# Retention and GELU MLP on one core: an opening with masks made on chip, earlier casts of v, and another order of loads

## The chip, the cores and the metric

The kernel runs on one core of a Trainium2 chip. The metric is device time in microseconds (us) of one execution; lower is better. Engines are called PE (TensorE matmul), PEld (its weight load), DVE (VectorE), ACT (ScalarE), POOL (GpSimd) and SP (SyncE, which here only issues DMAs).

## The reference

q, k, v are float32 of shape (4 batches, 8 heads, 768 positions, 64). With one decay per head, `gamma = 1 - 2**(-5 - h)`, the first part is a recurrence over positions:

```python
state = gamma * state + einsum('bhd,bhe->bhde', k[:, :, t], v[:, :, t])
y[:, :, t] = 0.125 * einsum('bhd,bhde->bhe', q[:, :, t], state)
```

y, as x of 3072 tokens by 512, goes through a two-layer network with w_in (512 x 2048) and w_out (2048 x 512):

```python
h = x @ w_in
g = 0.5 * h * (1 + tanh(sqrt(2 / pi) * (h + 0.044715 * h ** 3)))
out = g @ w_out
```

## The kernel before

**Chunks.** The positions are cut into six chunks of 128. Within a chunk and batch the recurrence becomes matrix products in float16: transposed q and k give scores (`mm_A`), the scores are multiplied by a triangular mask that also carries a factor per head (`ev_A`, DVE, line 267), the result times v plus the state's contribution gives y (`mm_yi`, `mm_yc`; copied to `xT` by `ev_Y`), and k times v updates the state (`mm_s`, `ev_S`). Powers of gamma are put into q and k while these are cast to float16 (`prep1`, line 177 on DVE or POOL; v is only cast, line 172 on ACT, 174 on POOL). `decay` scales a copy of the state on POOL.

**Two ways to the transposes.** For chunks 0 and 1, PE transposes q and k against an identity matrix (`mm_T`), and `ev_T` copies the result out of PSUM. From chunk 2 for q, and chunk 3 for k, the load itself puts blocks of 32 in place (`load_blk`, 16 DMAs), POOL scales them (`prep_blk`, line 188) and DVE transposes them (line 240).

**The network.** M1 (`moe1`, `moe1_two`, line 401) multiplies w_in by `xT` into banks with tag "h"; GELU on ACT (line 416) gives g. M2 (`moe2`, line 434) multiplies g by w_out; `ev_O` copies the output and sends it out. The eight PSUM banks are two for tag "h", two for "o", four for "att". M1 of chunk 0 is done by pairs of 128-wide column blocks (`fp` 0 to 3, for the token columns `t01` of batches 0 and 1, or the other half), and then by single blocks 8 to 15 for all tokens.

**Order.** The schedule is manual: on every engine and queue, instructions run in the order in which the program lists them. Loads of chunk 0 are issued from SP and ACT, weights from POOL's queue (`load_w_in`, five pieces; `load_w_out`, four), between POOL's `prep1` calls. In the opening PE also runs matmuls on zeros (`spin`). Line 500 builds the mask on DVE: eight `tensor_scalar` instructions that scale a triangle loaded as a constant; the identity matrix is loaded too. `hold` writes one element of the first q tile of chunk 1 from the third piece of w_out, so that chunk 1's loads on SP wait for that piece to land. M2 of chunk 0 is interleaved by hand with the attention of chunk 1, and so on: a dictionary says after which unit of matmul work which attention step is issued. `load(2)` issues chunk 2's loads on SP behind the output DMAs of chunk 0, k and v of each batch in turn; `prep(2, b)` on POOL does q, k, v of each batch in turn.

Of the kernel before, what the change touches and what calls it, by code (L numbers as in the profile page):

```python
# [10 lines left out]
F32 = mybir.dt.float32  # L11
AF = mybir.ActivationFunctionType
ALU = mybir.AluOpType
# [3 lines left out]
def kernel(  # L17
# [9 lines left out]
    nc = tc.nc  # L27
    B, H, S, Dh = q.shape
    C = 128
    NCk = S // C  # L30
    NHP = H // 2
# [8 lines left out]
    p_i = np.arange(128, dtype=np.float64)  # L40
    qdec = gam[None, :] ** (p_i[:, None] - 32.0) * 0.125
    kdec = gam[None, :] ** (160.0 - p_i[:, None])
    g128 = gam ** 128.0
    gst = np.where(p_i[:, None] < 64, g128[None, 0::2], g128[None, 1::2])
    tri = (p_i[:, None] <= p_i[None, :]).astype(np.float64)

    j_p, t_p = np.arange(128)[:, None] // 64, np.arange(128)[:, None] % 32
    hp_c, a_c = np.arange(16)[None, :] // 4, np.arange(16)[None, :] % 4
    g_t, t_t = gam[2 * hp_c + j_p], a_c * 32.0 + t_p
    qdec_t = g_t ** (t_t - 32.0) * 0.125  # L50
    kdec_t = g_t ** (160.0 - t_t)
    cst_np = np.concatenate([qdec, kdec, gst, tri, qdec_t, kdec_t], axis=1).astype(np.float32)
    cst_h = nc.inline_tensor(cst_np, name="rr_cst")
    iden_np = np.eye(128, dtype=np.float32).astype(np.dtype("float16"))
    iden_h = nc.inline_tensor(iden_np, name="rr_ident")

    ctx.enter_context(tc.manual_schedule())
    const = ctx.enter_context(tc.tile_pool(name="const", bufs=1))
# [5 lines left out]
    op = ctx.enter_context(tc.tile_pool(name="op", bufs=4))  # L64
    psum = ctx.enter_context(tc.tile_pool(name="psum", bufs=1, space=bass.MemoryType.PSUM))

    OQ, OK, OG, OT = 0, H, 2 * H, 2 * H + NHP
    OQT, OKT = OT + 128, OT + 144


    misc = const.tile([128, 32], F32)
    cst = const.tile([128, 192], F32)
    iden = const.tile([128, 128], F16)

    raw = {}
# [4 lines left out]
    BLK = {"q": (2, 3, 4, 5), "k": (3, 4, 5)}  # L80
# [20 lines left out]
    def load1(eng, nm, c, b):  # L101
        eng.dma_start(
            out=ld_tile(nm, c, b),
            in_=srcs[nm][b, :, c * C:(c + 1) * C, :].rearrange("h p d -> p h d"),
        )

    def load_blk(nm, c):
        t = ld_all((nm + ("32" if nm == "q" else "T32"), c))
        src = srcs[nm].rearrange("b (hp j) s (dd d) -> j dd s (b hp) d", j=2, dd=2)
        for j in range(2):  # L110
            for dd in range(2):
                for a in range(4):
                    p0, t0 = (2 * j + dd) * 32, c * C + a * 32
                    nc.sync.dma_start(
                        out=t[p0:p0 + 32, :, a, :], in_=src[j, dd, t0:t0 + 32]
                    )

    def load(c):
        for nm in "qk":
            if c in BLK[nm]:  # L120
                load_blk(nm, c)
        for b in range(B):
            for nm in "vk" if c in BLK["k"] else "kv":
                load1(nc.sync, nm, c, b)

    def hold(nm, c, b, until):

        nc.gpsimd.tensor_copy(out=ld_tile(nm, c, b)[0:1, 0, 0:1], in_=until)

    nc.sync.dma_start(out=cst[:, :OT], in_=cst_h.ap()[:, :OT])  # L130
    load1(nc.scalar, "q", 0, 0)
    load1(nc.sync, "k", 0, 0)
    load1(nc.scalar, "k", 0, 1)
    nc.sync.dma_start(out=iden, in_=iden_h.ap())
    nc.sync.dma_start(out=cst[:, OT:OKT + 16], in_=cst_h.ap()[:, OT:])
    load1(nc.sync, "q", 0, 1)
    load1(nc.scalar, "v", 0, 0)
    load1(nc.sync, "k", 0, 2)
# [4 lines left out]

    zero = const.tile([128, 512], F16, name="zero")
    nc.vector.memset(zero, 0.0)  # L145
    nc.scalar.activation(
        out=misc[:, 0:1], in_=zero[:, 0:1], func=AF.Gelu_apprx_tanh, scale=1.0
    )
# [7 lines left out]


    st = const.tile([128, NHP, B, 128], F16, name="st")
    nc.gpsimd.memset(st, 0.0)
    stg = const.tile([128, NHP, B, 128], F32, name="stg")  # L160

    h16 = {}
# [2 lines left out]
    def prep1(eng, nm, c, b):  # L165
        t = pre.tile(
            [128, H, Dh], F16, tag=f"{nm}16", bufs=6 if nm == "q" else 2 * B, name=f"{nm}16"
        )
        src = ld_tile(nm, c, b)
        if nm == "v":  # L170
            if eng is nc.scalar:
                eng.copy(out=t, in_=src)  # L172
            else:
                eng.tensor_copy(out=t, in_=src)  # L174
        else:
            col = OQ if nm == "q" else OK
            eng.tensor_tensor(  # L177
                out=t,
                in0=src,
                in1=cst[:, col:col + H].unsqueeze(2).broadcast_to([128, H, Dh]),  # L180
                op=ALU.mult,
            )
        h16[nm, c, b] = t
# [65 lines left out]
    def mm_A(c, b):  # L249
        t = qkT[c, b]  # L250
        ps = [bank("att", name=f"a_ps{j}") for j in range(2)]
        for hp in range(NHP):
            for j in range(2):
                nc.tensor.matmul(  # L254
                    out=ps[j][:, hp],
                    lhsT=t[j * 64:(j + 1) * 64, 1, hp],
                    rhs=t[j * 64:(j + 1) * 64, 0, hp],
                    start=True,
                    stop=True,
                )  # L260
        pss["A", c, b] = ps

    def ev_A(c, b):
        ps = pss.pop(("A", c, b))
        for j in range(2):
            s = att.tile([128, NHP, 128], F16, tag=f"a{j}", name=f"a_sb{j}")
            nc.vector.tensor_tensor(out=s, in0=ps[j], in1=mask[:, j], op=ALU.mult)  # L267
            a_sb[c, b, j] = s
# [173 lines left out]
    def moe2(c, b, fcs, tag="o"):  # L442
        if fcs[0] == 0:
            o_ps[c, b] = bank(tag, shape=(128, d_model), name="o_ps")
        moe2_mm(o_ps[c, b], c, b, fcs, 0, d_model)

    def ev_O(c, b):
        ps = o_ps[c, b]
        rows = out[b * S + c * C:b * S + (c + 1) * C, :]
        o_sb = op.tile([128, d_model], F32, tag="o", name="o_sb")  # L450
        if b == B - 1 and c > 0:
            nc.vector.tensor_copy(out=o_sb, in_=ps)
        else:
            nc.scalar.copy(out=o_sb, in_=ps)  # L454
        if c == NCk - 1:
            eng = nc.scalar
        else:
            eng = nc.sync if c == 0 and b < B - 1 else nc.gpsimd
        eng.dma_start(out=rows, in_=o_sb)  # L459

    def moe2_last(c, b):
# [31 lines left out]
    ev_T(0, 0, AC)  # L493
    load1(AC, "v", 0, 2)
    prep1(VE, "q", 0, 1)

    mask = const.tile([128, 2, NHP, 128], F32, name="mask")
    for j in range(2):
        for hp in range(NHP):
            nc.vector.tensor_scalar(  # L500
                out=mask[:, j, hp],
                in0=cst[:, OT:OT + 128],
                scalar1=float(1.0 / g128[2 * hp + j]),
                scalar2=None,
                op0=ALU.mult,
            )

    prep1(PO, "k", 0, 1)

    load_w_in(0)  # L510
    prep1(PO, "k", 0, 2)
    prep1(PO, "q", 0, 2)
    for i in range(1, len(w_in_n)):
        load_w_in(i)
    prep1(PO, "k", 0, 3)
# [7 lines left out]
    prep1(AC, "v", 0, 0)  # L523
    spin(3)
    mm_A(0, 1)
    ev_A(0, 1)
    mm_yc(0, 0, "o")
    mm_yi(0, 0)
# [20 lines left out]
    moe1_two(0, 0, *t01)  # L549
    mm_s(0, 1, "o")  # L550
    mm_A(0, 3)
    ev_A(0, 3)
    moe1_two(0, 1, *t01)
    ev_S(0, 1, AC)
    prep1(AC, "v", 0, 2)
    prep1(AC, "v", 0, 3)
    mm_yc(0, 2, "o")
    mm_yi(0, 2)
    ev_Y(0, 2, AC)
    mm_yc(0, 3, "o")  # L560
    mm_yi(0, 3)
    ev_Y(0, 3)
    mm_s(0, 2)
    mm_s(0, 3)
    moe1_two(0, 2, *t01)
    moe1_two(0, 3, *t01)
    ev_S(0, 2)
    ev_S(0, 3)
    for fp in range(4):
        moe1_two(0, fp, half, 2 * half)  # L570
    for b in range(B):
        decay(0, b)
# [42 lines left out]
    )  # L615


    load(2)
    for b in range(B):
        prep(2, b)  # L620
    run(
        [
            (lambda fp=fp, t=t: moe1_two(1, fp, *t))
# [88 lines left out]
```

## Time and profile before

| | us |
|---|---|
| median of 13 runs | 220.49 |
| lowest, highest of them | 220.11, 223.24 |
| the profiled execution | 220.9 |
| its span, first to last instruction | 218.6 |
| PE busy in the span | 208.5 |
| DVE, ACT, POOL busy | 85.9, 87.0, 97.4 |
| matmuls of M1 (line 401), of M2 (line 434) | 86.3, 88.1 |
| mean granted clock of PE | 0.99 of full |

Times within the span count from its first instruction. A matmul row's mean includes the pipeline's depth, so that eight matmuls of 256 columns with a row mean near 300 ns take 0.87 us in a sequence. An idle time is put down to the event that ended it, its releaser. A DMA has two times: that of its issue on a queue, and that until its data has landed.

### The profile page before, as it was taken

To read this page: it belongs to the slowest core of one execution; us is meant where nothing else is said; L and a number is where in the kernel's file an instruction comes from. 1 tells how busy PE (TensorE), PEld (TensorE's weight loads), DVE (VectorE), ACT (ScalarE), POOL (GpSimd) and SP (SyncE) were. 2 spreads that over 40 slices of the span, in tenths; PEclk is the share of its full clock that TensorE was granted. 3 is DMA by queue.
4 is the path that set the end of the run, shared out by engine and by line. 5 is a ranking of instruction groups with operands and counts; after the bars stand their busy time and mean duration, and the time that the engine had idled before them with its cause. 6 is when DMAs were issued, how large, how long until landed. Compare 5 with 4: busy or idle time off the path is not lost.

```text
span 218.6 us, 3898 instructions
## 1 busy us (share of the span) xinstructions
PE 208.5 (95%) x1535; PEld 114.3 (52%) x1535; DVE 85.9 (39%) x152; ACT 87.0 (40%) x148; POOL 97.4 (45%) x117
## 2 busy tenths in 40 slices
PE   7869699999999999999999999999999999999992
PEld 2436574445888765444455444545444545444462
DVE  1484500129954761432781433691353660100001
ACT  2424677142456333176313175314266223466120
POOL 4895320330469613499714699510399411000000
PEclk9969999999999999999999999999999999999999
DMA  7999999996699779998769987489920011200111
GB/s 163 288 232 206 206 207 254 218 267 137 136 220 221 116 120 196 230 268 134 110 133 195 268 192 113 78 157 222 252 82 3 0 48 61 86 0 0 51 76 68
DMA packets 125089, 32.88 MB, mean 150 GB/s; under 512 B 118224, under 2 KB 123216, under 8 KB 125072
## 3 DMA queue, kind: packets, MB, share of 16 engines
q1 hardware_dynamic: 108128, 20.58, 47.8%
q0 software_dynamic: 6112, 8.65, 17.1%
q10 hardware_dynamic: 10832, 3.41, 6.3%
q8 instruction: 12, 0.20, 0.4%
q14 instruction: 5, 0.04, 0.1%
HBM read 30.53 MB, written 6.29 MB: 168 GB/s over the span
## 4 chain that ended last, share of the span: by engine, by line
PE 89%; DVE 3%; DMA 3%; issue 1%; ACT 1%; SPq 1%; DVEq 0%
PE h_ps L401 38%; PE o_ps L434 37%; PE y_ps L289 3%; PE a_ps L254 3%; DMA q<-in_q_dram 3%; PE s_ps L308 2%; PE y_ps L276 2%; PE qkT_ps L231 2%; DVE mask L500 1%; PE spin_ps L153 1%; DVE q L177 1%; ACT v L172 1%; DVE a_sb L267 0%; DVE qkT L215 0%; ACT st L213 0%
## 5 line engine op out<-in xcount | busy, mean ns | idle before, releaser
L434 PE MATMUL o_ps<-w_out,g 128*128 128x512 f16 (+1 forms) x400 | 88.1, 371 | 0.0
L401 PE MATMUL h_ps<-xT,w_in 128*128 128x512 f16 (+1 forms) x480 | 86.3, 337 | 0.0
L416 ACT ACTIVATE g<-h_ps 128x512 f16<-128x512 f32 x96 | 57.3, 597 | 49.9 <-PE h_ps L401 49.9
L401 PEld LDWEIGHTS <-w_in 128*128 128x128 f16 x480 | 46.1, 98 | 35.7
L434 PEld LDWEIGHTS <-g 128*128 128x128 f16 x400 | 37.7, 98 | 38.8
L267 DVE TENSOR_TENSOR a_sb<-a_ps,mask 128x512 f16<-128x512 f32 x48 | 30.6, 691 | 18.5 <-PE a_ps L254 18.4
L177 POOL TENSOR_TENSOR k<-k,cst 128x512 f16<-128x512 f32 x24 | 24.9, 1039 | 15.2 <-DMA k<-in_k_dram 15.2
L459 POOL DMA_DIRECT2D out_dram<-o_sb x17 | 9.7, 568 | 47.6 <-ACT o_sb L454 38.0
L454 ACT COPY o_sb<-o_ps 128x512 f32<-128x512 f32 x19 | 11.1, 586 | 45.8 <-PE o_ps L434 37.2
L334 POOL TENSOR_TENSOR stg<-st,cst 128x512 f32<-128x512 f16 x16 | 16.4, 1037 | 20.6 <-DVE st L325 14.0
L325 DVE TENSOR_TENSOR st<-s_ps,stg 64x256 f16<-64x256 f32 x32 | 13.5, 421 | 17.8 <-PE s_ps L308 17.2
L188 POOL TENSOR_TENSOR q<-q,cst 128x512 f16<-128x512 f32 x16 | 16.7, 1043 | 2.4 <-DMA k<-in_k_dram 2.4
L240 DVE STREAM_TRANSPOSE qkT<-q 128x512 f16<-128x512 f16 x16 | 11.2, 698 | 11.5 <-POOL q L188 11.4
L213 ACT CAST xT<-y_ps 128x512 f16<-128x512 f32 x15 | 8.3, 588 | 16.6 <-PE y_ps L289 16.6
L177 DVE TENSOR_TENSOR q<-q,cst 128x512 f16<-128x512 f32 x7 | 6.0, 858 | 17.5 <-DMA q<-in_q_dram 17.5
L188 POOL TENSOR_TENSOR kT<-kT,cst 128x512 f16<-128x512 f32 x12 | 12.5, 1042 | 0.0
L153 PE MATMUL spin_ps<-zero 128*128 128x512 f16 x31 | 10.8, 499 | 1.2 <-DVE zero L145 1.2
L254 PE MATMUL a_ps<-qkT 64*128 64x128 f16 x192 | 8.5, 220 | 2.7 <-DVE a_sb L267 1.9
L289 PE MATMUL y_ps<-a_sb,v 128*64 128x128 f16 x192 | 8.9, 226 | 2.1 <-ACT v L172 2.0
L471 DVE COPY o_sb<-o_ps 128x256 f32<-128x256 f32 x1 | 0.4, 425 | 25.2 <-PE o_ps L434 25.2
L174 POOL CAST v<-v 128x512 f16<-128x512 f32 x16 | 9.6, 601 | 0.0
L215 DVE CAST xT<-y_ps 128x512 f16<-128x512 f32 x9 | 5.9, 686 | 9.3 <-PE y_ps L289 9.3
(33 smaller groups left out, 98.2 us busy)
## 6 DMA issues: line engine op xcount, KB each, us to landing
k<-in_k_dram SPq DMA_DIRECT2D x22, 256.0 KB, 4.6
v<-in_v_dram SPq DMA_DIRECT2D x18, 256.0 KB, 4.6
out_dram<-o_sb POOLq DMA_DIRECT2D x17, 256.0 KB, 3.5
q<-in_q_dram SPq DMA_DIRECT2D x64, 64.0 KB, 2.6
kT<-in_k_dram SPq DMA_DIRECT2D x48, 64.0 KB, 2.7
w_out<-in_moe_w_out_dram POOLq DMA_DIRECT2D x4, 512.0 KB, 15.6
v<-in_v_dram ACTq DMA_DIRECT2D x6, 256.0 KB, 5.4
q<-in_q_dram SPq DMA_DIRECT2D x6, 256.0 KB, 5.5
```

What stands on the lines that cost most here:

```text
L153: nc.tensor.matmul(out=ps, lhsT=zero[:, 0:128], rhs=zero, start=True, stop=True)
L177: eng.tensor_tensor(out=t, in0=src, in1=cst[:, col:col + H].unsqueeze(2).broadcast_to([128, H, Dh]), op=ALU.mult,)
L188: nc.gpsimd.tensor_tensor(out=t, in0=ld_all((key, c))[:, b * NHP:(b + 1) * NHP].rearrange("p hp a d -> p (hp a) d"), in1=cst[:, col:col + ...
L240: nc.vector.transpose(out=t[:, i].rearrange("p hp t -> p (hp t)"), in_=blk16.pop((nm, c, b)).rearrange("p ha d -> p (ha d)"),)
L254: nc.tensor.matmul(out=ps[j][:, hp], lhsT=t[j * 64:(j + 1) * 64, 1, hp], rhs=t[j * 64:(j + 1) * 64, 0, hp], start=True, stop=True,)
L267: nc.vector.tensor_tensor(out=s, in0=ps[j], in1=mask[:, j], op=ALU.mult)
L289: nc.tensor.matmul(out=y_ps[j * 64:(j + 1) * 64, hp], lhsT=h16["v", c, b][:, 2 * hp + j], rhs=a_sb[c, b, j][:, hp], start=(c == 0), stop=True,
L325: eng.tensor_tensor(out=st[sl, :, b, sl], in0=s_ps[sl, :, sl], in1=stg[sl, :, b, sl], op=ALU.add,)
L334: nc.gpsimd.tensor_tensor(out=stg[:, :, b], in0=st[:, :, b], in1=cst[:, OG:OG + NHP].unsqueeze(2).broadcast_to([128, NHP, 128]), op=ALU.mult,)
L401: nc.tensor.matmul(out=out, lhsT=w_in_sb[wi][:, kc, wr * 128:(wr + 1) * 128], rhs=xT[c][:, kc, t0:t1], start=(kc == 0), stop=(kc == NHP - ...
L416: nc.scalar.activation(out=out, in_=in_, func=AF.Gelu_apprx_tanh, scale=1.0)
L434: nc.tensor.matmul(out=ps[:, n0:n1], lhsT=g_sb[c, fc // 2][:, fc % 2, b * C:(b + 1) * C], rhs=w_out_sb[fc // (NF // NO)][:, fc % (NF // NO ...
```

## The change

It has five parts.

1. **Constants.** The triangle and the identity matrix are no longer loaded. DVE fills `iden` with ones and the eight parts of `mask` with their factors by `memset`; POOL's `affine_select` then zeroes what is off the diagonal or below it, one instruction for `iden` and one for the whole mask of 128 x 1024. The remaining constants come in one DMA. `st` is zeroed on DVE instead of POOL.
2. **q of batch 2, chunk 0,** is scaled on DVE, ahead of `ev_A` of batch 1, instead of on POOL.
3. **v of batches 2 and 3, chunk 0.** Both casts stood on ACT behind the second GELU and the state copy of batch 1. Now v of batch 3 is cast on ACT right behind the first GELU, and v of batch 2 on DVE ahead of `ev_A` of batch 3. `ev_Y` of batches 2 and 3 trade engines.
4. **M1 of batch 2.** M1 of the columns of batches 2 and 3 for `fp` 0 and 1 is done for each of the two batches apart (`t2`, `t3`). That of batch 2 stands ahead of `fp` 2 of the first half.
5. **Chunk 2.** The output DMAs of chunk 0, batches 0 to 2, are collected in `late`. SP issues q blocks, then k of all batches, then these outputs, then v. POOL scales q and k of all batches before it casts v.

```diff
-    nc.sync.dma_start(out=cst[:, :OT], in_=cst_h.ap()[:, :OT])
+    nc.sync.dma_start(out=cst[:, :OKT + 16], in_=cst_h.ap())
...
-    nc.sync.dma_start(out=iden, in_=iden_h.ap())
-    nc.sync.dma_start(out=cst[:, OT:OKT + 16], in_=cst_h.ap()[:, OT:])
...
+    mask = const.tile([128, 2, NHP, 128], F32, name="mask")
+    nc.vector.memset(iden, 1.0)
+    for j in range(2):
+        for hp in range(NHP):
+            nc.vector.memset(mask[:, j, hp], float(1.0 / g128[2 * hp + j]))
+    nc.gpsimd.affine_select(out=iden, in_=iden, pattern=[[1, 128]],
+        base=0, channel_multiplier=-1, compare_op=ALU.is_equal, fill=0.0)
+    nc.gpsimd.affine_select(
+        out=mask.rearrange("p j hp t -> p (j hp) t"),
+        in_=mask.rearrange("p j hp t -> p (j hp) t"),
+        pattern=[[0, 2 * NHP], [1, 128]],
+        base=0, channel_multiplier=-1, compare_op=ALU.is_ge, fill=0.0)
...
-    nc.gpsimd.memset(st, 0.0)
+    nc.vector.memset(st, 0.0)
...
+        if c == 0 and b < B - 1:
+            late.append((rows, o_sb))
+            return
...
-    mask = const.tile([128, 2, NHP, 128], F32, name="mask")
-    for j in range(2):
-        for hp in range(NHP):
-            nc.vector.tensor_scalar(out=mask[:, j, hp], in0=cst[:, OT:OT + 128],
-                scalar1=float(1.0 / g128[2 * hp + j]), scalar2=None, op0=ALU.mult)
     prep1(PO, "k", 0, 1)
     load_w_in(0)
     prep1(PO, "k", 0, 2)
-    prep1(PO, "q", 0, 2)
...
     mm_A(0, 1)
+    prep1(VE, "q", 0, 2)
     ev_A(0, 1)
...
     moe1_two(0, 0, *t01)
     mm_s(0, 1, "o")
     mm_A(0, 3)
+    prep1(AC, "v", 0, 3)
+    prep1(VE, "v", 0, 2)
     ev_A(0, 3)
+    ev_S(0, 1, AC)
     moe1_two(0, 1, *t01)
-    ev_S(0, 1, AC)
-    prep1(AC, "v", 0, 2)
-    prep1(AC, "v", 0, 3)
     mm_yc(0, 2, "o")
     mm_yi(0, 2)
-    ev_Y(0, 2, AC)
+    ev_Y(0, 2)
+    mm_s(0, 2)
+    mm_s(0, 3)
     mm_yc(0, 3, "o")
     mm_yi(0, 3)
-    ev_Y(0, 3)
-    mm_s(0, 2)
-    mm_s(0, 3)
+    ev_Y(0, 3, AC)
+    moe1_two(0, 0, *t2)
+    moe1_two(0, 1, *t2)
     moe1_two(0, 2, *t01)
-    moe1_two(0, 3, *t01)
     ev_S(0, 2)
     ev_S(0, 3)
-    for fp in range(4):
+    moe1_two(0, 3, *t01)
+    moe1_two(0, 0, *t3)
+    moe1_two(0, 1, *t3)
+    for fp in range(2, 4):
         moe1_two(0, fp, half, 2 * half)
...
-    load(2)
+    load_blk("q", 2)
     for b in range(B):
-        prep(2, b)
+        load1(SY, "k", 2, b)
+    for rows, o_sb in late:
+        nc.sync.dma_start(out=rows, in_=o_sb)
+    for b in range(B):
+        load1(SY, "v", 2, b)
+    for b in range(B):
+        prep_blk("q", 2, b)
+        prep1(PO, "k", 2, b)
+    for b in range(B):
+        prep1(PO, "v", 2, b)
```

More of the change, by code (lines that the diff above doesn't have):

```diff
@@ L44 @@
     gst = np.where(p_i[:, None] < 64, g128[None, 0::2], g128[None, 1::2])
-    tri = (p_i[:, None] <= p_i[None, :]).astype(np.float64)
     j_p, t_p = np.arange(128)[:, None] // 64, np.arange(128)[:, None] % 32
@@ L51 @@
     kdec_t = g_t ** (160.0 - t_t)
-    cst_np = np.concatenate([qdec, kdec, gst, tri, qdec_t, kdec_t], axis=1).astype(np.float32)
+    cst_np = np.concatenate([qdec, kdec, gst, qdec_t, kdec_t], axis=1).astype(np.float32)
     cst_h = nc.inline_tensor(cst_np, name="rr_cst")
-    iden_np = np.eye(128, dtype=np.float32).astype(np.dtype("float16"))
-    iden_h = nc.inline_tensor(iden_np, name="rr_ident")
     ctx.enter_context(tc.manual_schedule())
@@ L65 @@
     psum = ctx.enter_context(tc.tile_pool(name="psum", bufs=1, space=bass.MemoryType.PSUM))
-    OQ, OK, OG, OT = 0, H, 2 * H, 2 * H + NHP
-    OQT, OKT = OT + 128, OT + 144
+    OQ, OK, OG, OQT, OKT = 0, H, 2 * H, 2 * H + NHP, 2 * H + NHP + 16
     misc = const.tile([128, 32], F32)
-    cst = const.tile([128, 192], F32)
+    cst = const.tile([128, 64], F32)
     iden = const.tile([128, 128], F16)
@@ L122, in load @@
         for b in range(B):
-            for nm in "vk" if c in BLK["k"] else "kv":
+            for nm in "vk":
                 load1(nc.sync, nm, c, b)
@@ L145 @@
     nc.vector.memset(zero, 0.0)
+    mask = const.tile([128, 2, NHP, 128], F32, name="mask")
[4 more added lines that the diff above has]
+    nc.gpsimd.affine_select(
+        out=iden,
+        in_=iden,
+        pattern=[[1, 128]],
+        base=0,
+        channel_multiplier=-1,
+        compare_op=ALU.is_equal,
+        fill=0.0,
+    )
+    nc.gpsimd.affine_select(
+        out=mask.rearrange("p j hp t -> p (j hp) t"),
+        in_=mask.rearrange("p j hp t -> p (j hp) t"),
+        pattern=[[0, 2 * NHP], [1, 128]],
+        base=0,
+        channel_multiplier=-1,
+        compare_op=ALU.is_ge,
+        fill=0.0,
+    )
     nc.scalar.activation(
@@ L445, in moe2 @@
         moe2_mm(o_ps[c, b], c, b, fcs, 0, d_model)
+    late = []
     def ev_O(c, b):
@@ L454, in ev_O @@
             nc.scalar.copy(out=o_sb, in_=ps)
[L455 to L458, printed above, removed]
+        if c == 0 and b < B - 1:
+            late.append((rows, o_sb))
+            return
+        eng = nc.scalar if c == NCk - 1 else nc.gpsimd
         eng.dma_start(out=rows, in_=o_sb)
@@ L495 @@
     prep1(VE, "q", 0, 1)
-    mask = const.tile([128, 2, NHP, 128], F32, name="mask")
-    for j in range(2):
-        for hp in range(NHP):
[L500 to L506, printed above, removed]
     prep1(PO, "k", 0, 1)
```

## The prediction

> **What bounds the kernel now.** I read the page first, then the chain that ended last, then the waits of TensorE, then stretches of time. The page says that TensorE (PE) is busy for 95% of the span, and its slices say where the rest is:
>
> ```profile
> PE   7869699999999999999999999999999999999992
> PEclk9969999999999999999999999999999999999999
> ```
>
> All gaps lie in the first five slices of 5.5 us, and slice 3 runs at a lower granted clock. The stretches settle it (columns: stretch, its length, busy us and instruction count of PE, PEld, DVE, ACT, POOL, then clock, DMA share, GB/s):
>
> ```profile
> 8.40:12.90 4.50, 1.87 (x20) 0.95 (x21) 4.44 (x10) 1.53 (x2) 3.67 (x5) 1.00 1.30 255
> 12.90:17.00 4.10, 4.08 (x38) 2.54 (x37) 2.95 (x4) 1.32 (x3) 4.10 (x6) 0.58 1.35 237
> 22.00:25.45 3.45, 1.38 (x26) 1.12 (x27) 0.85 (x2) 2.94 (x6) 1.04 (x1) 1.00 1.24 206
> 25.45:214.80 189.35, 189.19 (x1377) 103.76 (x1374) 73.47 (x130) 75.96 (x129) 81.37 (x96) 1.00 0.67 143
> ```
>
> From 25.45 us PE is busy 189.19 of 189.35 us: that part can only be moved, not shortened. PE idles 2.6 us in 8.4 to 12.9 and 2.1 us in 22 to 25.45, and between them works at clock 0.58. TensorE's waits and the chain name the causes:
>
> ```profile
> PE y_ps L289 <- ACT v L172: 2.0, 1, 2.0
> PE a_ps L254 <- DVE a_sb L267: 1.9, 1, 1.9
> ```
> ```profile
> 8.28 0.69 DVE q L177
> 8.97 1.45 DVE mask L500 x5
> 10.42 0.86 issue
> 11.29 1.55 DVE mask L500 x3
> 12.84 0.04 DVE a_sb L267
> ```
>
> The first scores were ready at 8.8, but VectorE (DVE) built the eight mask pieces until nearly 12.8, so `a_sb` and the next score matmul waited. Later v of batches 2 and 3 was cast on ScalarE (ACT) only at 23.29, behind two GELUs and a state copy. The bound is thus an order of work on DVE and ACT in the opening; behind it lie landings, since the DMA share is above 1 in every stretch from 8.4 to 25.45.
>
> **What the Trainium skill says.** "SBUF — State Buffer", Who interferes with whom: VectorE's `tensor_scalar` in a 2-port mode and GpSimd (POOL) lock each other out. The trace fits: the masks' median is 220 ns, the longest 1284 ns, and the 0.86 us gap lies inside POOL's multiply of 10.24 to 11.27. The same section says that an instruction with at most one SBUF input outside those modes doesn't contend; no row shows a `memset` beside POOL's reads. "VectorE: DVE Perf Modes", Zero memsets can be issued as uint32: one cycle per element; `zero`, 256 words, took 0.27 us, which agrees and gives 1.05 ns an element. "DMA: Bandwidth & Descriptors", Queues, rings and completion order: the engines take turns between queues. In 15 to 16 us the trace has POOL's queue at 85.0% and SP's at 53.7% of 16 engines' time, so the weights' queue takes a large share once it runs. "TensorE: Matmul & The Clock Gate", Part 1: the clock is halved after an idle window; 0.58 after the first gap agrees, while the second gap lowered nothing.
>
> **The change, part by part.** Times are us of the span of this profiled execution.
>
> *Transfers.* SP's constants shrink from 10 + 32 + 80 KB to 128 x 52 x 4 bytes = 27 KB: 95 KB, at the 287 GB/s of this stage 0.33 us for all that follows. q of batch 1 stood behind them; k of batch 0 landed at 1.13 + 4.0 = 5.1 and q at 8.25. Two full queues have about half each, 256 KB per 1.8 us, so q lands near 7.0.
>
> *DVE.* The eight mask scalings (8.97 to 12.84) go. In come memsets of `iden` (128 elements, 0.13), eight masks (0.13 each, 1.1) and `st` (1024 words, 1.08): 2.3 us, with 60 ns apiece for start 2.9, from 1.13 to some 4.0. The first q landed at 3.9; its product is needed only when the 14 spins end at 6.66, so this is hidden with 2 us to spare.
>
> *POOL.* The `st` memset (1.80 us) goes, two `affine_select` come. No row shows one. Per element the nearest rows are the cast (0.60 us for 512) and the multiply (1.04 for 512): 1.2 to 2.1 us for the mask's 1024, 0.15 to 0.3 for `iden`. I take 2.1 + 0.3. It starts when the memsets are done, at 2.6, and ends by 5.0; POOL's first multiply waits for k until 5.25. Cost nothing; each us by which it is slower delays k, and all behind it, by one, and from below nothing is to be had.
>
> *q of batch 2* moves from POOL (1.03) to DVE (0.69, or 1.07 beside POOL as q of batch 3 shows). POOL then issues the last four `w_in` DMAs right after k of batch 2, near 9.5 and not 11.23; `w_out` follows earlier too. On DVE it lands at 3.04 + 7.0 = 10.0, just as DVE is done with `a_sb` of batch 0, and delays `a_sb` of batch 1 by 0.7, while PE has spins.
>
> *The walk with these.* Score matmul of batch 0 at 8.4 as before; `a_sb` 8.8 to 10.1 (two of 0.65); transposes of batch 1 right behind the scores, their copy on ACT to 10.2; scores of batch 1 at 10.2; v cast to 10.8; y of batch 0 at 10.9 (before: 13.4). q of batch 2 to 10.8, `a_sb` of batch 1 to 12.1, transposes of batch 2 at 12.1 (15.9), y of batch 1 at 12.5 (16.7), scores of batch 2 at 14.1 (18.2). No gap over 0.5 us, so I take the clock as full. Now landings rule: q of batch 3 came at 7.13 + 7.7 = 14.8, v of 2 at 8.27 + 7.1 = 15.4, v of 3 at 8.19 + 8.1 = 16.3, the second `w_in` at 11.23 + 6.4 = 17.6. I leave q at 15.0, let both v slip by up to 1 us for the earlier weights, and the second `w_in` come before 17. Then on DVE: q of 3 to 15.7, `a_sb` of 2 to 17.0, the copy of the last transposes (0.68) to 17.7, v of 2 to 18.1 (a cast that DVE doesn't show: half to all of ACT's 0.62), `a_sb` of 3 to 19.4. PE: transposes of 3 at 15.7 (19.0), first M1 pair, scores of 3 at 17.7, second M1 pair to 18.9, y of 2, two state matmuls, y of 3 at 19.7, M1 unbroken from 20.1, when `xT` of batch 2 is there. Before: 25.45. **Gain 5.35 us**: 3.3 from the mask and its slow clock (transposes of 3), 2.05 from the casts.
>
> *v of 3 ahead of the state copy and the second GELU* delays both by 0.62 on ACT. Behind that GELU stands only M1's next use of its bank, which is later. *y of batches 2 and 3* trade engines: 0.69 on DVE and 0.58 on ACT, as before.
>
> *M1 of batch 2 ahead.* 16 matmuls of 256 columns become 32 of 128: 0.22 us for 4 against 0.87 for 8, the same time. GELUs of 256 elements: 0.20 us for one element and 0.60 for 512 give 0.40, beside 0.44 of PE. Cost nothing (at most 0.2); they fill the wait for `xT` of batch 3.
>
> *Chunk 1.* M2 then starts at 32.3, not 37.6. Its loads don't move so far: they are held until the third `w_out`, 16.9 + 16.6 = 33.5. The first transposes would be due at 46.9 - 5.3 = 41.6; k landed at 34.02 + 6.1 = 40.1, with 1.04 us of POOL 41.2. Covered by 0.4 us; the other three batches have more (the last k is ready at 49.2, due at 50.4). ACT's v loads start earlier, out of the way of q and k. Instead, ACT's third v load now waits for k of batch 1 (q before), with the evictions of M2's output queued behind it; their bank is wanted only four units later. I charge 0.2 (0 to 1.5).
>
> *Chunk 2.* POOL's first multiply was at 62.23, while the first transposes would be due at 66.6 - 5.3 = 61.3: unchanged loads would cost 3 us. The new order issues q right behind k of chunk 1 (43 instead of 49.48), past the three output DMAs on SP. Those then leave near 56; their buffers are next written past 70. POOL does q and k ahead of v, and starts near 55. Cost and gain nothing, but it guards the gain. Chunk 3's loads only start sooner.
>
> Sum: -5.35 + 0.2 = -5.15. The profiled execution took 220.9 (span 218.6 and 2.3 around it), 0.41 above the median of 220.49; so 215.7 for it, 215.3 for the median.
>
> **Rivals.** *A, the forecast* (0.70): M1 unbroken between 18.7 and 21.7, 213.9 to 216.9.
> *B, the loads take part back* (0.17): four weight DMAs start 1.7 us sooner while q and v of batches 2 and 3 are still under way, and at the shares of 15 to 16 us these lose half their rate; each then slips 2 us or more, M1 starts near 22.5, or chunk 1's k comes 2 us late. 217.5. For it: DMA is never idle there. Against it: the bytes are the same, and M1 needed the weights anyway.
> *C, slower* (0.07): the select is a slow operation on POOL. Its end is 2.6 plus its length; over 2.6 us delays the first k, and with it transposes and weights. The gain is gone at about 7.8 us, 7.6 ns an element, nearly four times the multiply's; at 10 us the time is 222.7. Nothing in the profile excludes it.
> *D, no change* (0.06): the gain only moves the wait, with PE standing before the transposes of chunk 1 or 2. It would take a landing 5 us later than due: about 220.
>
> **The numbers.** About 0.5%, 1.1 us, can be told from no change. Faster takes A, B and a part of D: 0.89. Same 0.04, slower 0.07. Range 213.9 to 218.0: A and most of B.
>
> **What would show it.** Right: no wait of scores for `a_sb`, no slice at 0.6 clock, y of batch 0 near 11, M1 unbroken near 20, a select below 2.6 us, under 0.5 us of PE idle at 40 to 50. Wrong: POOL's first k multiply past 6; v casts waiting for DMA past 18; a new wait of chunk 1's transposes for k.

## The result, and the profile after

The changed kernel takes 216.48 us (median of 11 runs, 215.98 to 218.35), the kernel before 220.66 (48 runs). The ratio is 0.984, 95% interval 0.982 to 0.986; it compares undisturbed executions only, so it is not the quotient of these medians. The profiled execution took 215.98 us with a span of 214.2, against 220.9 and 218.6 before: 4.4 us less in the span. Part of this is the clock of that one execution of the kernel before; the last section says how much.

The page of the changed kernel, busy tenths and granted clock in 40 slices:

```profile
PE   7898999989999999999999999999999999999992
PEclk9999999999999999999999999999999999999998
```

The slice at clock 0.6 is gone, and so are the two 6s of PE in slices 3 and 5. An 8 has appeared in slice 9 (42.8 to 48.2). The stretches of time (stretch, length, busy us and count of PE, PEld, DVE, ACT, POOL, clock, DMA share, GB/s); the first two are those of before:

```profile
8.40:12.90 4.50, 3.92 (x50) 2.26 (x48) 3.78 (x6) 3.36 (x5) 4.32 (x6) 1.00 1.32 260
12.90:17.00 4.10, 3.50 (x42) 2.25 (x40) 2.76 (x5) 2.03 (x6) 4.09 (x6) 1.00 1.33 230
19.42:32.20 12.78, 12.52 (x101) 8.18 (x98) 1.50 (x4) 8.54 (x16) 2.04 (x2) 1.00 1.24 205
41.70:51.74 10.04, 9.17 (x110) 5.84 (x108) 7.64 (x13) 5.48 (x10) 3.46 (x4) 1.00 0.98 200
51.74:210.10 158.36, 158.35 (x1146) 86.00 (x1143) 62.80 (x112) 61.91 (x105) 74.95 (x89) 1.00 0.62 136
```

In 8.4 to 12.9 PE now works 3.92 us and not 1.87, and in 12.9 to 17 the clock is 1.00 and not 0.58. Not all is gain. The fourth stretch is chunk 1 from its first transposes to its M1. It took 10.04 us, and PE stood for 0.87 of it. Before, the same stretch had hardly a gap, and what followed it was as long as now:

```profile
46.93:56.43 9.50, 9.36 (x109) 5.70 (x108) 8.20 (x13) 4.48 (x8) 1.38 (x2) 1.00 0.64 150
56.43:214.80 158.37, 158.35 (x1146) 86.07 (x1143) 62.80 (x112) 61.91 (x105) 74.65 (x89) 1.00 0.60 131
```

TensorE's waits in the changed kernel (engine, line, waited for: us, times, longest):

```profile
PE spin_ps L171 <- DVE zero L139: 1.3, 1, 1.3
PE o_ps L452 <- ACT o_sb L474: 0.9, 1, 0.9
PE h_ps L419 <- DMA w_in<-in_moe_w_in_dram: 0.8, 1, 0.8
PE a_ps L272 <- ACT qkT L231: 0.7, 2, 0.5
PE h_ps L419 <- ACT g L434: 0.2, 1, 0.2
```

Both waits that carried the forecast, for `a_sb` and for v, are gone. New are 0.9 us for `o_sb` in chunk 1 and 0.8 for the second piece of `w_in`. Four rows of the timeline (start, length, engine and operation, in brackets the idle time before and what ended it):

```profile
1.42 0.29 POOL L146 TENSOR_SCALAR_AFFINE_SELECT iden<-iden 128x128 f16<-128x128 f16 x1 [0.91 <-DVE iden L142]
2.54 1.09 POOL L155 TENSOR_SCALAR_AFFINE_SELECT mask<-mask 128x1024 f32<-128x1024 f32 x1 [0.83 <-DVE mask L145]
...
43.27 0.62 ACT L190 CAST v<-v 128x512 f16<-128x512 f32 x1 [10.28 <-issue]
...
44.43 1.02 PE L452 MATMUL o_ps<-w_out,g 128*128 128x512 f16 x4 [0.87 <-ACT o_sb L474]
```

The select of the mask took 1.09 us and was done at 3.6, well ahead of k at 5.0. The last two rows are the new stall. ACT was idle for 10.28 us, at the end of it because its next instruction was a DMA that waited: in the chain that ended last, k of batch 1 lands at 42.12 and ACT issues its v loads from 42.20. Behind these stood the v cast and the copies to `o_sb`, and behind a copy PE.

The gain can be followed at four stations. They are the start of M1 unbroken, of M2 of chunk 0, of M1 of chunk 1 and of M2 of chunk 1. From the last one to the end all profiles agree within 0.5 us (144.5 to 144.9), but for one, told of below. Each station is that of the profiled execution:

| kernel | M1, chunk 0 | M2, chunk 0 | M1, chunk 1 | M2, chunk 1 | span | median (runs) | ratio to before, 95% |
|---|---|---|---|---|---|---|---|
| before | 25.29 | 37.44 | 56.43 | 74.08 | 218.6 | 220.66 (48) | |
| after | 19.42 | 32.20 | 51.74 | 69.39 | 214.2 | 216.48 (11) | 0.984, 0.982 to 0.986 |
| part 1 undone | 20.39 | 33.17 | 52.24 | 69.89 | 214.8 | 216.70 (4) | 0.987, 0.981 to 0.993 |
| part 2 undone | 19.11 | 32.19 | 52.09 | 70.56 | 215.4 | 216.14 (4) | 0.981, 0.975 to 0.987 |
| part 3 undone | 22.27 | 35.62 | 54.24 | 71.89 | 217.7 | 219.38 (20) | 0.996, 0.993 to 0.999 |
| part 4 undone | 20.17 | 32.33 | 52.05 | 69.69 | 214.5 | 216.54 (4) | 0.985, 0.979 to 0.991 |
| part 5 undone | 19.48 | 32.26 | 51.59 | 71.36 | 216.2 | 218.26 (20) | 0.991, 0.989 to 0.994 |
| part 1 alone | 21.78 | 33.92 | 52.54 | 70.84 | 215.5 | 217.59 (4) | 0.986, 0.980 to 0.991 |
| part 2 alone | 23.02 | 36.66 | 55.28 | 72.92 | 217.5 | 219.20 (11) | 0.992, 0.988 to 0.995 |
| select five times | 23.79 | 36.57 | 55.19 | 72.83 | 217.4 | 218.60 (5) | 0.989, 0.984 to 0.994 |
| v of chunk 1 on SP | 19.60 | 32.47 | 51.08 | 69.33 | 214.2 | 216.00 (4) | 0.979, 0.975 to 0.984 |
| M1 of batch 3 in "o" | 19.61 | 31.80 | 52.52 | 70.17 | 215.0 | 217.08 (4) | 0.984, 0.979 to 0.990 |
| these two, earlier loads | 19.68 | 31.88 | 52.09 | 70.90 | 215.7 | 216.98 (6) | 0.983, 0.977 to 0.988 |
| "o", less v loaded | 19.45 | 31.64 | 50.69 | 68.34 | 212.8 | 214.76 (6) | 0.976, 0.970 to 0.981 |

From before to after: M2 of chunk 0 starts 5.24 sooner (5.87 at the start of M1, 0.63 given back within it), chunk 1 gives back 0.55, the stretch behind it nothing, and the tail behind the last matmul 0.3. Together that is 4.4.

### The profile page after: what moved, and what is told of

It is laid out like the page before. It is cut to its first block, busy times and chain, and to the rows that moved or that the text cites. A ratio compares the mean times of both kernels' runs of the same rounds, so it can differ in the third digit from the quotient of the medians.

```text
span 214.2 us, 3935 instructions
## 1 busy us (share of the span) xinstructions
PE 206.1 (96%) x1551; PEld 113.6 (53%) x1551; DVE 85.3 (40%) x156; ACT 86.5 (40%) x149; POOL 96.6 (45%) x117
## 3 DMA queue, kind: packets, MB, share of 16 engines
q0 software_dynamic: 6112, 8.65, 17.6%
q10 hardware_dynamic: 10832, 3.41, 6.7%
## 4 chain that ended last, share of the span: by engine, by line
PE 77%; DMA 14%; POOL 3%; SPq 3%; ACT 1%; issue 1%; ACTq 0%; DVE 0%
PE o_ps L452 34%; PE h_ps L419 33%; DMA w_out<-in_moe_w_out_dram 9%; DMA k<-in_k_dram 5%; PE y_ps L307 3%; PE a_ps L272 3%; SPq L98 2%; PE y_ps L294 2%; PE s_ps L326 2%; POOL w_in L400 1%; PE qkT_ps L249 1%; POOL k L195 1%; DMA out_dram<-o_sb 1%; POOL w_out L409 1%; ACTq L98 0%
## 5 line engine op out<-in xcount | busy, mean ns | idle before, releaser
L419 PE MATMUL h_ps<-xT,w_in 128*128 128x512 f16 (+2 forms) x496 | 86.7, 331 | 1.1 <-DMA w_in<-in_moe_w_in_dram 0.8
L434 ACT ACTIVATE g<-h_ps 128x512 f16<-128x512 f32 (+1 forms) x98 | 57.5, 588 | 48.5 <-PE h_ps L419 48.4
L285 DVE TENSOR_TENSOR a_sb<-a_ps,mask 128x512 f16<-128x512 f32 x48 | 30.1, 682 | 16.7 <-PE a_ps L272 16.5
L343 DVE TENSOR_TENSOR st<-s_ps,stg 64x256 f16<-64x256 f32 x32 | 13.5, 421 | 17.8 <-PE s_ps L326 17.2
L231 ACT CAST xT<-y_ps 128x512 f16<-128x512 f32 x15 | 8.3, 588 | 12.2 <-PE y_ps L307 12.2
L171 PE MATMUL spin_ps<-zero 128*128 128x512 f16 x31 | 9.2, 439 | 1.3 <-DVE zero L139 1.3
L190 ACT CAST v<-v 128x512 f16<-128x512 f32 x7 | 4.3, 621 | 11.6 <-issue 10.3
L258 DVE STREAM_TRANSPOSE qkT<-kT 128x512 f16<-128x512 f16 x12 | 8.3, 689 | 1.8 <-POOL kT L206 1.8
```

The costliest lines, as they stand in the source:

```text
L258: nc.vector.transpose(out=t[:, i].rearrange("p hp t -> p (hp t)"), in_=blk16.pop((nm, c, b)).rearrange("p ha d -> p (ha d)"),)
L343: eng.tensor_tensor(out=st[sl, :, b, sl], in0=s_ps[sl, :, sl], in1=stg[sl, :, b, sl], op=ALU.add,)
L419: nc.tensor.matmul(out=out, lhsT=w_in_sb[wi][:, kc, wr * 128:(wr + 1) * 128], rhs=xT[c][:, kc, t0:t1], start=(kc == 0), stop=(kc == NHP - ...
L434: nc.scalar.activation(out=out, in_=in_, func=AF.Gelu_apprx_tanh, scale=1.0)
```

## The experiments

### Where the 3.3 us of the mask were

**Part 1 undone** (the triangle and the identity are loaded, DVE scales the masks, POOL zeroes `st`):

```diff
-    nc.vector.memset(iden, 1.0)
...
     prep1(VE, "q", 0, 1)
+    mask = const.tile([128, 2, NHP, 128], F32, name="mask")
+    for j in range(2):
+        for hp in range(NHP):
+            nc.vector.tensor_scalar(out=mask[:, j, hp], in0=cst[:, OT:OT + 128], ...
```

> The changed kernel with part 1 undone: triangle and identity are loaded, DVE scales the eight mask parts, POOL zeroes st; parts 2 to 5 stay. Theory O (order of work: the mask alone is worth what the prediction gave it): +3.3 us against the changed kernel, 219.8, with PE idle near 11 waiting for a_sb and a slice of lower clock. Theory L (landings: the changed opening stands at the second and third w_in piece at 17.2 and 20.3 us, so that part of the mask's time is slack by now): +1.0 to 2.5 us, 217.5 to 219, with M1 unbroken from 20.5 to 22.

M1 starts only 0.97 later, chunk 1's M2 0.50. DVE's timeline of this kernel:

```profile
8.64 2.25 DVE L502 TENSOR_SCALAR mask<-cst 128x128 f32<-128x128 f32 x8
```

The same eight instructions took 3.95 us in the kernel before. What is missing now beside them is POOL's multiply of q of batch 2. In the kernel before, POOL ran two multiplies without a break beside the masks (9.23 to 11.27) and then issued `w_in`; here it ran one (8.98 to 10.02), and then issued `w_in`. PE waits 0.7 us for `a_sb` and not 1.9, and 12.9 to 17 runs at clock 1.00.

**Part 2 alone**, on the kernel before:

```diff
-    prep1(PO, "q", 0, 2)
...
     mm_A(0, 1)
+    prep1(VE, "q", 0, 2)
```

> The kernel before with part 2 alone: q of batch 2 is scaled on DVE ahead of ev_A of batch 1, not on POOL. Theory O: the masks stay on DVE's path, at most the 0.86 us gap goes and 0.7 us of DVE comes in: 0 to -0.5 us. Theory K: the eight masks take 2.3 us and not 3.95 (as with part 1 undone), the PE stall falls from 1.9 to 0.7 us, the clock stays full and the later w_in pieces are issued 1.3 us sooner: -1.5 to -2.5 us, nearly what part 1 brings.

The masks take 2.27 us here too, so it is the place of the multiply and not something else of the change. The last three masks of the kernel before and of this one (count: shortest, median, longest in ns; first and last start in us):

```profile
L500 DVE TENSOR_SCALAR mask<-cst x3: 211/213/1284, 11.3 to 11.6; 128x128 f32<-128x128 f32 x3
L500 DVE TENSOR_SCALAR mask<-cst x3: 215/453/521, 10.5 to 10.8; 128x128 f32<-128x128 f32 x3
```

Most masks take 0.22 us. In the kernel before, two were stretched, to 1.07 us (from 9.29) and 1.08 (from 10.28), each beside one of POOL's two multiplies, and the last to 1.28, while POOL issued `w_in` (from 11.23). Here one is stretched to 1.08 beside the one multiply left, and the last two to 0.52 and 0.45 beside the issue of `w_in` (from 10.32). So about half of the 1.7 us saved is the second multiply, and the rest is the end, where the masks met the issue; no run parts the two.

M1 starts 2.3 sooner. But behind the wait for v the clock fell to half (22.67 to 26.08 us), and M1 took 13.64 us in place of 12.15; of the 2.3, 1.2 was left at chunk 1's M2. What sets off such a fall is told in the last section.

**Part 1 alone**, on the kernel before (the constants' lines of the change's diff, nothing else):

> The kernel before with part 1 alone (mask and identity made on chip, st zeroed on DVE); q of batch 2 stays on POOL, everything else as before. Theory O: the mask is worth 3.3 us at the transposes of batch 3; chunk 2's loads, unchanged, give about 1 back: -2.3 us or more, 218. Theory K (the mask was slow because POOL's multiply of q of batch 2 locks VectorE out; making masks on chip and moving that multiply each cure the same stall): also -2 to -2.5 us. Neither gain nor loss would say that the opening's first half is hidden by landings.

M1 starts 3.5 sooner; the ratio is a gain of 1.4%, against 1.6% for the whole change, and the two intervals overlap. The wait for v stays as it was, in TensorE's waits of this kernel:

```profile
PE y_ps L307 <- ACT v L190: 2.0, 1, 2.0
...
PE qkT_ps L249 <- POOL k L195: 0.7, 2, 0.5
```

Of the second row, 0.5 us are at the transposes of chunk 2, the wait that part 5 removes; the other 0.2 are in the opening.

**Part 2 undone** (q of batch 2 is multiplied on POOL again, ahead of the last four `w_in` DMAs):

```diff
     prep1(PO, "k", 0, 2)
+    prep1(PO, "q", 0, 2)
...
-    prep1(VE, "q", 0, 2)
```

> The changed kernel with part 2 undone: q of batch 2 back on POOL behind k of batch 2; parts 1, 3, 4, 5 stay. Theory K (the multiply's harm was that it locked VectorE out of the mask; with the mask made early there is nothing left to lock): +0 to +0.4 us, the 1.03 us of POOL only makes the second w_in piece's issue later, near 10.6, and its landing was bound by the transfers. Prediction's reading (w_in issued 1.7 us sooner is worth having): +0.5 to +1.0 us, with PE's wait for w_in growing from 0.8 to 1.5 us or more.

Nothing is lost in the opening: M2 starts at 32.19 against 32.20, though `w_in` is issued 1.1 us later. The profiled execution was the slowest of the four by 1 us, with 0.6 of waiting for k of chunk 2; the median, 216.14, is at the changed kernel's.

So the stall in the kernel before needed both: the masks on DVE, and POOL's second multiply with the issue of `w_in` behind it. Either cure takes most of it, and the two don't add up.

### The casts of v

**Part 3 undone:**

```diff
-    prep1(AC, "v", 0, 3)
-    prep1(VE, "v", 0, 2)
     ev_A(0, 3)
-    ev_S(0, 1, AC)
     moe1_two(0, 1, *t01)
+    ev_S(0, 1, AC)
+    prep1(AC, "v", 0, 2)
+    prep1(AC, "v", 0, 3)
...
```

The state matmuls and `ev_Y` of batches 2 and 3 go back to their old places too.

> The changed kernel with part 3 undone: both v casts on ACT behind the second GELU and the state copy, the state matmuls and ev_Y as before; parts 1, 2, 4, 5 stay. Theory O: +2.05 us, 218.5, PE idle some 2 us in front of y of batch 2. Theory L: the second GELU itself waits for the second w_in piece at 17.2 us, so the casts end near 20.4 and M1 is unbroken from 21.5: the same +2 us. Less than 1 us would speak against both.

The wait is back as it was before, in PE's timeline:

```profile
20.35 1.16 PE L307 MATMUL y_ps<-a_sb,v 128*64 128x128 f16 x16 [1.97 <-ACT v L190]
```

Behind it the clock is at half (20.46 to 23.87 us). M1 starts 2.85 later, and the lowered clock makes it 0.57 longer (13.35 us against 12.78). At chunk 1's M2, 2.5 us are left, since the `o_sb` wait is not there. The ratios differ by 1.2%, 2.6 us. The span shows 3.5, but 1.0 of that lies behind the last matmul, where this profile alone has 5.1 us and the changed kernel's 4.1.

### The split of M1

**Part 4 undone** (M1 of the second half in one piece, ahead of nothing):

```diff
-    moe1_two(0, 0, *t2)
-    moe1_two(0, 1, *t2)
     moe1_two(0, 2, *t01)
+    moe1_two(0, 3, *t01)
...
-    for fp in range(2, 4):
+    for fp in range(4):
```

> The changed kernel with part 4 undone: no M1 of batch 2 ahead, pairs of 256 columns only; parts 1, 2, 3, 5 stay. Prediction's reading (the split costs nothing and fills the wait for xT of batch 3): slower by 0.4 to 0.9 us. Theory L: 0.6 us of GELU turn-around between half-size banks goes, but fp 2 of the first half then stands at w_in piece 3, which lands at 20.3 while y of batch 3 is done at 19.4: +0.3 us (0 to 0.5), with a PE wait for w_in of 0.9 us. If neither holds and the split was a pure cost: -0.6 us.

```profile
20.17 4.00 PE L419 MATMUL h_ps<-xT,w_in 128*128 128x256 f16 x35 [0.40 <-DMA w_in<-in_moe_w_in_dram]
```

In PE's timeline M1 waits for the third piece of `w_in` and starts 0.75 later, but then takes 12.16 us and not 12.78. M2 starts 0.13 later. The split fills a wait for a landing and pays nearly the same within M1, the 0.24 us of waiting for a GELU to free a bank among it. Its ratio can't be told from the changed kernel's.

### Chunk 2's loads

**Part 5 undone:**

```diff
-    load_blk("q", 2)
-    for b in range(B):
-        load1(SY, "k", 2, b)
-    for rows, o_sb in late:
-        nc.sync.dma_start(out=rows, in_=o_sb)
...
+    load(2)
     for b in range(B):
-        prep1(PO, "v", 2, b)
+        prep(2, b)
```

> The changed kernel with part 5 undone: outputs of chunk 0 on SP ahead of chunk 2's q blocks, k and v of each batch in turn, POOL's q, k, v by batch. Prediction's reading: POOL's first multiply of chunk 2 stays near 62.2 us, while its transposes are due at 61.7: +3 us, 219.5. Rival: the outputs that SP waits for are evicted 3 us earlier too (the third at 45.3 and not 48.4), so that the q blocks move along, POOL starts near 59 and the last k is ready near 69, just when it is due: 0 to +0.7 us.

TensorE's waits and POOL's timeline of this kernel:

```profile
PE qkT_ps L249 <- POOL k L195: 2.4, 3, 1.4
```
```profile
60.98 1.05 POOL L206 TENSOR_TENSOR q<-q,cst 128x512 f16<-128x512 f32 x1 [5.80 <-PE h_ps L419]
```

Of the 2.4 us, 1.8 are at the transposes of chunk 2 and 0.6 in the opening. The releaser that the second row names is not what POOL waited for: in the chain of this kernel the multiply at 60.98 follows the landing of k at 60.63. Up to chunk 1's M1 this kernel is as early as the changed one (51.59). Then the transposes of chunk 2 start at 63.09, against 61.72, and M2 of chunk 1 1.97 later; the ratios differ by 0.75%, 1.7 us. Without the new order of loads, some 1.7 to 2 us of what the opening gained would have been given back 40 us later.

### A slower select

```diff
-    nc.gpsimd.affine_select(
+    for _ in range(5):
+        nc.gpsimd.affine_select(
```

> The changed kernel with the mask's affine_select issued five times over (the result is the same): 4 x 1.09 us more on POOL, which is then free at 8.0 us while k landed at 5.1. The prediction's rule for a slow select (each us past k's landing costs one us of the whole): +2.9 us, 219.4. Theory L: PE's first gap is made good while it would have waited for w_in (0.8 us) and by slack ahead of it, but w_in is issued later too: +1.5 to +2.5 us. Under 0.5 us: POOL's opening has slack all through.

POOL's timeline of this kernel, then a stretch of it:

```profile
2.54 6.39 POOL L156 TENSOR_SCALAR_AFFINE_SELECT mask<-mask 128x1024 f32<-128x1024 f32 x5 [0.83 <-DVE mask L145]
8.90 2.04 POOL L196 TENSOR_TENSOR k<-k,cst 128x512 f16<-128x512 f32 x2
```
```profile
8.40:12.90 4.50, 2.90 (x18) 1.32 (x19) 0.00 (x0) 1.01 (x1) 4.48 (x6) 0.52 1.28 288
```

The first k is multiplied 3.77 us later than in the changed kernel (8.90 against 5.13), as the prediction's rule has it. M1 starts 4.37 later, as PE stands for 3.4 us and then runs at half clock. Of this, 3.4 us are left at chunk 1's M2 in the profile, where the `o_sb` wait is gone, and 2.1 in the medians. The chain is the forecast one, but "one for one" is its upper end.

### What stands behind the gain now

**v of chunk 1 on SP.** The last two v loads of chunk 1 go to SP, between and behind the k loads, so that no DMA waits on ACT:

```diff
     load1(SY, "k", 1, 1)
+    load1(SY, "v", 1, 2)
...
     load1(SY, "k", 1, 3)
-    load1(AC, "v", 1, 2)
-    load1(AC, "v", 1, 3)
+    load1(SY, "v", 1, 3)
```

> The changed kernel with the loads of v of chunk 1, batches 2 and 3, issued by SP (behind k of batch 1 and behind the last k) instead of ACT. Theory Q (ACT stands in front of the third v load until k of batch 1 has landed near 42 us, and the outputs behind it come 0.9 us late for PE): that wait of M2 for ACT goes, -0.5 to -0.9 us, 215.7. Prediction's reading (their bank is wanted four units later, 0.2 us at most): no difference. Rival: k of batches 2 and 3 land later behind v on the same queue, +0.5 us, with a PE wait for POOL k.

The wait for `o_sb` is gone, which shows its cause, and the stage from the first transposes of chunk 1 takes 9.12 us, even less than before the change. In its place TensorE's waits have

```profile
PE qkT_ps L249 <- POOL k L195: 0.4, 1, 0.4
```

at the transposes of chunk 2, and M2 of chunk 1 starts at 69.33 against 69.39. The 0.66 won at M1 of chunk 1 is given up for k of chunk 2. Its median is 0.5 below the changed kernel's, and the two intervals overlap.

**M1 of batch 3 in the other banks.** It stands right behind that of batch 2, ahead of `fp` 2, in banks of tag "o" that are free at that time (`moe1_two` takes the tag as one more argument):

```diff
     moe1_two(0, 1, *t2)
+    moe1_two(0, 0, *t3, "o")
+    moe1_two(0, 1, *t3, "o")
     moe1_two(0, 2, *t01)
...
-    moe1_two(0, 0, *t3)
-    moe1_two(0, 1, *t3)
```

> The changed kernel with M1 of batch 3 (fp 0 and 1) moved ahead of fp 2, and put into the two idle banks of tag o. Theory L (M1 after y of batch 3 stands at w_in piece 3, 20.3 us, and at the turn-around of two half-used banks; together 0.6 us): M2 starts at 31.6 and not 32.2; chunk 1's first k is ready at 41.1, just when it is due, and the wait for ACT's outputs grows by what was won: 0 to -0.3 us in the whole, 216.3. Prediction's reading (the split costs nothing): no difference in M2's start.

M1 takes 12.19 us: with all the work for which weights were there in front, the wait of 0.24 us for a GELU is gone. M2 starts 0.40 sooner. But the stall of chunk 1 grows by more:

```profile
PE o_ps L452 <- ACT o_sb L474: 2.1, 1, 2.1
```

In TensorE's waits it is 2.1 us in place of 0.9, and M1 of chunk 1 starts 0.78 later than in the changed kernel.

**Both, with earlier loads.** Besides, the loads of chunk 1 are held only until the second piece of `w_out`:

```diff
-    hold("q", 1, 0, w_out_sb[2][0:1, 0, 0:1])
+    hold("q", 1, 0, w_out_sb[1][0:1, 0, 0:1])
```

> The changed kernel with three edits: v of chunk 1, batches 2 and 3, loaded by SP; M1 of batch 3 ahead of fp 2 in the banks of tag o; chunk 1's loads released by the second piece of w_out instead of the third. Theory Q+L (what is left after the change is ACT's wait for k of chunk 1 and the landings of chunk 1 and 2, which the earlier release moves ahead by 2 us, while w_out has over 3 us to spare): M2 at 31.7, no wait for ACT, no wait for chunk 2's k: -1.2 us, 215.2 (214.9 to 215.8). Rival (the transfers are saturated, an earlier release only delays w_out): a PE wait for w_out in M2, no gain over loads on SP alone, 216.0 or more.

```profile
PE h_ps L419 <- ACT xT L231: 1.4, 1, 1.4
...
PE qkT_ps L249 <- POOL k L195: 1.0, 1, 1.0
```

The waits in this kernel lie elsewhere, but they are there: 1.4 us for `xT`, whose copy stands on ACT behind a v cast that waits for its landing (3.32 us of ACT's idle time ended by v at 50.45), and 1.0 for k of chunk 2. It ends no earlier than the changed kernel.

**Fewer bytes.** As "M1 of batch 3 in the other banks", and v of batches 2 and 3 of chunk 1 is left out: it is not loaded, and v of batches 0 and 1 is cast in its place:

```diff
-        src = ld_tile(nm, c, b)
+        src = ld_tile(nm, c, b - 2 if nm == "v" and c == 1 and b > 1 else b)
...
-    load1(AC, "v", 1, 2)
-    load1(AC, "v", 1, 3)
```

> As m1_o, but v of chunk 1, batches 2 and 3, is not loaded: v of batches 0 and 1 is cast in its place, so this computation is left out and 0.5 MB of transfers with it (some 1.8 us at 285 GB/s), and ACT has no load to wait for. Theory W (after the change the transfers of chunks 1 and 2 are the wall: m1_o and the three-edit kernel won 0.4 us at M2 and lost it again at chunk 1's or 2's landings): with fewer bytes the wall moves, no wait for ACT, no PE wait for k of chunk 2, M2 of chunk 1 starts near 68.6 and not 69.4: 215.3 to 215.8. Rival (the order on the engines bounds, not the bytes): the same as loads on SP, 216.0 or more, with a new wait between 42 and 69 us that is for an engine and not for a landing.

All that is left of TensorE's waits:

```profile
PE spin_ps L171 <- DVE zero L139: 1.3, 1, 1.3
PE a_ps L272 <- ACT qkT L231: 0.7, 2, 0.5
```

With 0.5 MB less, the 0.56 us won by M2 of chunk 0 becomes 1.05 at both stations of chunk 1, and the time 214.76. This run takes away two things together, the bytes and the DMA that blocked ACT. Taking away the second alone, on SP, moved chunk 1's M2 by 0.06. That points to the transfers of chunks 1 and 2 as what holds the rest: with all bytes, whatever was won ahead of them was lost again to a landing, in three tries. Whether the other banks and the loads on SP would keep a part together without the earlier loads was not run. No version that does the whole work beat the changed kernel by more than the intervals.

## Why the prediction was right, and where not

The forecast was 5.15 us less for the profiled execution; the span became 4.4 less. Its own steps:

- **The bound** held. The order of work on DVE and ACT in the opening was what PE waited for; with parts 1 and 3 neither wait nor the low clock is left. The walk was near: y of batch 0 at 10.30 (10.9 forecast), of batch 3 at 19.07 (19.7), M1 at 19.42 (20.1), M2 at 32.20 (32.3), the first transposes of chunk 1 at 41.69 (41.6). That M2 fits so well is in part luck: M1 began 5.87 sooner than before, not 5.35, and then took 0.63 longer.
- **"3.3 from the mask and its slow clock"** was mis-sized as the price of part 1. The prediction saw that the gap in the masks lay inside POOL's multiply, cited the lock between `tensor_scalar` and POOL (the Trainium skill, "SBUF — State Buffer", Who interferes with whom), and still put all 3.3 on the masks. Part 1 alone moves M1 by 3.5, but with part 2 in place it is worth only 0.97 there. The trace agrees with the lock: 3.95 us for the eight masks beside two multiplies, 2.25 and 2.27 beside one. One reading was off: the longest mask, 1.28 us, lies beside the issue of `w_in`, and what the chain shows as a gap of 0.86 is a mask of 1.08. And a part of the 3.3 is a window of half clock, which this execution had and a few others, by their mean clock, did not (last section).
- **"2.05 from the casts"** was too small: M1 moves by 2.85, and 2.5 to 2.6 reaches the end. The wait itself is 2.0; most of the rest is the clock behind it, which the prediction took as untouched since it had been so in the one profile that it had.
- **"q of 2 lets `w_in` be issued 1.7 sooner"**: it was issued 1.66 sooner, and the second piece landed 0.4 sooner (17.2 us, when PE's wait for it ended, against 17.6), the last not at all (12.2 us from issue to landing became 13.5). The slip of v was 0.7, within the 1 us allowed. q of batch 3 came at 12.1 and not at 15.0, unforecast.
- **The split, "cost nothing (at most 0.2)"**: M1 became 0.63 longer. It filled a wait of about the same size, so the net is nothing, but not for the reason given. Without it PE waited for the third piece of `w_in`, not for `xT` of batch 3; with it PE waits 0.24 for a GELU to free a bank.
- **Chunk 1, "I charge 0.2 (0 to 1.5)"**: 0.55. The mechanism was named, ACT's third v load waits for k with evictions behind it. The step that failed is "their bank is wanted only four units later": PE wanted it 0.87 us before the copy was done. With it went one of the signs of being right, under 0.5 us of PE idle at 40 to 50.
- **Chunk 2, "would cost 3 us"**: 1.97 at chunk 1's M2. The loads did come later than PE, but POOL's first multiply would have moved from 62.23 to 60.98 by itself, as what stands ahead of the loads on SP was done earlier.
- **The select**: 1.09 us for the mask, half of the 2.1 taken, and 0.29 for `iden`. It was hidden, as forecast.
- **The sum**: of the 0.75 missing in the span, 0.11 lies ahead of M2, 0.35 in chunk 1 and 0.3 in the tail behind the last matmul. That tail, which holds the last copies and output DMAs, was 3.8 before, 4.1 after and 5.1 in the run without part 3; no run explains it. The median is 1.2 above the forecast, more than the span accounts for: 215.98, the profiled execution, was the lowest of the 11, where the one before lay 0.41 above its median.

Of the rivals, B (loads) took nothing at the opening; D is real in small, as the `o_sb` wait. C was excluded by the select's 1.09 us.

## What to carry to other kernels

Before a stall is priced, look at what each of its sides would do alone: here the masks and a neighbour's multiply made one stall together, and either cure took most of it. When an early stage is shortened, follow the gain to the next landings and to each engine that issues a DMA which may have to wait: what stands behind that DMA waits with it. Part 5 earned nothing of its own and kept 1.7 to 2 us. And a wait of TensorE can cost more than its length: whether the clock falls behind it can differ between two executions of one kernel, so a single profile does not price it.

## What was not expected of the hardware

- **Same gap, other clock.** The wait for v is 1.97 us in four profiles. In the kernel before and with part 1 alone the clock stayed full, and M1 took 12.15 and 12.14 us; without part 3 and with part 2 alone it fell, and M1 took 13.35 and 13.64. What decides can be read from the kept traces. They record the granted clock in stretches, and in each of the 14 profiles the borders of these lie whole multiples of 3.41 us apart; where they lie in the program differs (the first one recorded between 3.92 and 6.89 us). Cut at these borders, stretches (columns as above: behind its length, PE's busy time; the third from the end is the clock) of the kernel before (first three), part 1 alone, part 3 undone (two) and part 2 alone are:

```profile
9.58:12.99 3.41, 1.01 (x10) 0.27 (x8) 3.31 (x7) 1.53 (x2) 3.41 (x5) 1.00 1.31 241
12.99:16.40 3.41, 3.41 (x27) 2.05 (x27) 2.91 (x4) 1.10 (x2) 3.41 (x5) 0.50 1.34 244
19.82:23.23 3.41, 2.18 (x26) 1.56 (x24) 2.00 (x4) 1.77 (x4) 0.30 (x1) 1.00 1.23 203
19.31:22.72 3.41, 2.16 (x33) 1.82 (x34) 1.26 (x3) 2.15 (x5) 1.04 (x1) 1.00 1.24 206
17.04:20.46 3.42, 1.45 (x21) 0.99 (x22) 1.29 (x2) 2.44 (x6) 1.74 (x2) 1.00 1.24 207
20.46:23.87 3.41, 3.41 (x40) 3.05 (x39) 2.22 (x5) 1.33 (x3) 1.08 (x2) 0.50 1.24 206
19.26:22.67 3.41, 1.33 (x24) 0.80 (x23) 0.81 (x3) 2.94 (x6) 1.04 (x1) 1.00 1.25 206
```

In the kernel before and with part 1 alone a border splits the gap (at 23.23 and 19.31); in the other two the gap lies inside one window. In all 14 profiles, a window at full clock in which PE was busy for 1.45 us or less was followed by one at half clock, and a window with 1.58 or more never was. So the limit lies near 45% of busy time in a window of 3.41 us. The Trainium skill ("TensorE: Matmul & The Clock Gate", Part 1) puts an idle window at some 3.4 us; the length agrees, but here such a window need not be idle all through.
- **What that is worth.** A window at half clock takes 0.008 off the mean granted clock of a span (3.41 x 0.5 / 218.6). The executions of the kernel before with which the experiments are compared lie in such steps: at a mean of 0.998 and above they took 218.3 to 218.8 us (3 of them), near 0.99 218.9 to 221.4 (38), near 0.98 221.3 to 222.3 (10), at 0.975 222.9 (2). The changed kernel took 215.98 to 216.64 at 0.995 and above (10), and 218.35 at 0.992 (1). So of its 4.2 us in the median about 2 are there at full clock, and about 2 are windows of half clock that the shorter gaps no longer bring. This is read from the means alone; only the profiled executions show where a window lay. Without part 3 it is alike: 217.9 to 218.4 at 0.993 and above (4), 218.9 to 220.3 at 0.989 and below (16).
- **`affine_select`** on POOL: 1.09 us for 1024 float32 a partition, 1.06 ns an element; in a row of five 1.28 us each; 0.29 us for 128 of float16.
- **`memset`** on DVE: 0.165 us for 128 elements of float32 a partition, 0.27 for 256 words and 0.91 for 1024. The three give 0.83 ns an element and 0.06 us for the start (an estimate from them), where the prediction took 1.05 ns.
- **The opening's 14 spins** took 4.49 us in the run without part 5, where the first recorded border lay at 3.92 us, and 5.96 with v of chunk 1 on SP, where it lay at 6.89: 0.43 us apiece ahead of the border. The work behind them began at 5.58 and 7.05, M1 at 19.48 and 19.60: what was lost or won there was gone by then, since landings and DVE set the start of M1.
